# Attention chunks of 448 tokens, MLP blocks apart from them, and the last two MLP blocks beside each other

## The chip, the core and the metric

The kernel runs on one core of a Trainium2 chip. The metric is the device time of one execution in microseconds (us); before the change the median of three runs is 1187.18 us (1186.54 to 1188.1). TensorE (PE in the profile) multiplies, VectorE (DVE) and ScalarE (ACT) work on tiles element by element, GpSimd (POOL) helps a little, and SyncE (SP) issues the DMAs. Each engine works through its own instructions strictly in the order in which the program wrote them.

## The reference, cut to what matters

Batch 2, 3136 tokens each (6272 in all), 256 model columns. Three steps follow each other: an attention whose scores are squared and not normalised, an MLP with a convolution of three taps along the tokens, and a second MLP behind a LayerNorm.

```python
attn = np.maximum(z @ z.T / S, 0.0) ** 2          # z: 64 columns
x = u * (attn @ v)
h = np.maximum(x @ w_in, 0.0)                     # 1024 columns
c = conv_w[0]*h[t-1] + conv_w[1]*h[t] + conv_w[2]*h[t+1]
y = (h * sigmoid(c)) @ w_out
out = y + np.maximum(layernorm(y) * g_ln @ w_ch1, 0.0) @ w_ch2
```

## The kernel before, in words

Every float32 operand is split into a high and a low part that TensorE takes at full rate (`ah` and `al`, `vh` and `vl`, `gh` and `gl`), and a product is three matmuls: high by high, low by high, high by low.

The tokens are cut twice by `plan()` (L260). A *block* is what an MLP works on: 15 blocks of three tiles of 128 tokens and two of two tiles (`SIZES`). A *chunk* is what the attention works on; before the change there is one chunk per block, ending two tokens past it (the convolution needs one more token on either side), with exceptions at the border of the batches. The 17 chunks are 386, 384 six times, 446, 322, 384 six times, 256 and 256 wide.

Per chunk `c`, the attention goes through 25 tiles `j` of keys. `scores()` (L588) issues two matmuls into a PSUM bank of tag `w`; ACT takes the relu (L608) and the square (L617), or DVE squares (L613); ACT or DVE writes `ah` (L381, L385), DVE writes `al` (L626). `av()` (L648) then issues six matmuls (L658, L660, L661, for two halves of the columns) into the accumulator `av`. So a key tile costs eight matmuls of the chunk's width, and the last one six. `make_x()` (L669) multiplies by `u` and splits the result into `xh`, `xl`.

`mlps()` (L715) is one block: for each of eight slices `k` of the 1024 columns six matmuls into `hps` (L738 to L740), then relu, three taps, sigmoid and gate on ACT and DVE (L771 to L817), the split into `gh`, `gl`, and three matmuls of 256 columns per tile into the accumulator `y` (L754 to L756). After the eighth slice come the LayerNorm (ACT copy `ysb` L832, then DVE L837 to L872 with one power on POOL), the transposes `tps` (L884), and the second MLP with the same matmul counts (`h2ps`, `g2h`, `g2l`, `y`), a residual sum (L925) and the DMA out. The weights come in as 64-bit words and are decoded in 16 pieces of 512 columns (and a small one for the taps) by `decode()` (L477): about eight passes on DVE each, and three steps that ACT or POOL does between them.

What stands in which order is decided when the program is built. Every operation gets a due time; `Program.order()` (L144) plays the engines through with the prices of `PRICE` (L45), and each engine always takes the ready operation with the earliest due time whose buffers are free. `LAG0`, `LAG1` say how far an MLP's due times lie behind its chunk; `BESIDE` puts off the second MLP of the last block but one by 35 us.

Of the kernel before, what the change touches and what calls it, by code (L numbers as in the profile page):

```python
# [8 lines left out]
F32 = mybir.dt.float32  # L9
F32R = mybir.dt.float32r  # L10
U32 = mybir.dt.uint32
# [248 lines left out]
def plan():  # L260

    ends, t = [], 0
    for n in SIZES:
        t += n * P
        ends.append(t)
    assert t == NT
    chunks, blocks, q0, s = [], [], 0, 0  # L270
    for e in ends:
        q1 = NT if e == NT else e + 2
        if q0 < S < q1 or (q1 < S and S - q1 < 256):
            q1 = S
        if q1 == NT and q1 - q0 < 256:
            q0 = q1 - 256
            assert q0 >= s
        chunks.append((q0, q1))
        blocks.append((s, e))
        q0, s = q1, e  # L280
    return chunks, blocks
# [3 lines left out]
def attn_moe_kernel(ctx: ExitStack, tc: tile.TileContext, zt, ut, v, w_in, conv_w, w_out, g_ln, w1, w2, out):  # L285
    nc = tc.nc
    chunks, blocks = plan()
    NC = len(chunks)
# [3 lines left out]
    UW = max(q1 - s + 1 + (q1 == NT) for (_, q1), (s, _) in zip(chunks, blocks))  # L292
# [22 lines left out]
    def maker(tag, places, where, shape, dtype):  # L315
# [7 lines left out]
        for tag, places, where, shape, dtype in (  # L323
            ("zst", 2, pool, [P, 512], F32),
            ("st", 3, pool, [P, 1024], F32),
            ("wc", 2, pool, [P, 512], U32),
            ("wn", 2, pool, [P, 512], U32),
# [3 lines left out]
            ("a", 3, pool, [P, CW], F32),  # L331
# [13 lines left out]
            ("xtl", 1, pool, [P, 2 * BW], F32R),  # L345
            ("bst", 2, pool, [P, NTT, 6], F32),
# [222 lines left out]
    def head(c):  # L569

        return chunks[c][0] - blocks[c][0] + 1
# [97 lines left out]
    def make_x(c):  # L669
        q0, q1 = chunks[c]  # L670
        n, o = q1 - q0, head(c)
        w = blocks[c][1] - blocks[c][0] + 2
        u, b = u_b[c], av_b[c]
        xh, xl = x_b[c] = buf("xh", True), buf("xl", True)

        def half(t, d, a, e):
            return at(t).rearrange("p (k t) -> p k t", k=2)[:, d, a:e]
# [4 lines left out]
        if c == 0:  # L682
            op([("POOL", 0.15)], lambda e: nc.gpsimd.memset(edge(u, 0, 1), 0.0), writes=[(u, "head")], name="edge")
        else:
            k = head(c - 1) + chunks[c - 1][1] - chunks[c - 1][0]
            op(
                [("DVE", 0.09 + 0.0005 * 2 * o)],
                lambda e: nc.vector.tensor_copy(edge(u, 0, o), edge(u_b[c - 1], k - o, k)),
                reads=[(u_b[c - 1], 0), (u_b[c - 1], 1)], writes=[(u, "head")], name="edge", port=True,
            )  # L690
        keys = [(u, "head")]
        if q1 == NT:
            op([("POOL", 0.15)], lambda e: nc.gpsimd.memset(edge(u, o + n, o + n + 1), 0.0), writes=[(u, "tail")], name="edge")
            keys.append((u, "tail"))
        for d in range(2):
# [6 lines left out]
            )  # L702
        for d in range(2):
            op(
                ways_copy(w, "ACT"), lambda e, d=d: copy_r(e, half(xh, d, 0, w), half(u, d, 0, w)),
# [4 lines left out]
                lambda e, d=d: nc.vector.tensor_tensor(half(xl, d, 0, w), half(u, d, 0, w), f(half(xh, d, 0, w)), ALU.subtract),  # L710
                reads=[(u, d), (xh, d)] + keys, writes=[(xl, d)], name="xl", port=True,
            )


    def mlps(c, when):  # L715
        q0, q1 = chunks[c]
# [28 lines left out]
        def down(acc, nm, k, gh, gl, due):  # L745
            for i in range(ntt):

                def mm(e, i=i):
                    p = at(acc, "y").rearrange("p a b -> p (a b)")[:, i * D : (i + 1) * D]
# [4 lines left out]
                    nc.tensor.matmul(p, a, wh, start=first(acc, i // 2), stop=False, **kw)  # L754
# [5 lines left out]
                    adds=[(acc, i)], due=due + 0.3 * i, name=f"y{c}.{k}{nm}",  # L760
                )

        acc = buf("av", True) if last else buf("y", True)
# [60 lines left out]
        y = buf("u", True) if last else buf("ysb", True)  # L824
        bst, mv, ve, r, q = (buf(x) for x in ("bst", "mv", "ve", "rs", "rq"))

        def rows(i):
            return at(y)[:, i * D : (i + 1) * D]
# [39 lines left out]
        for i in range(ntt):  # L868
# [6 lines left out]
                reads=[(y, 0), (mv, i), (r, 1)], writes=[(xn, 0)], name="xn", port=True,  # L875
            )
            xns.append(xn)
        th, tl = (buf("xh", True), buf("xl", True)) if last else (buf("xth", True), buf("xtl", True))
        for d in range(2):
            ps = buf("w", kind="m")  # L880

            def turn(e, d=d, ps=ps):
# [10 lines left out]
                reads=[(ps, 0), ("gt",)], writes=[(th, d)], name="xth",  # L893
# [10 lines left out]
        acc2 = buf("y", True)  # L904
        for k in range(NF):
            ps = buf("w", kind="m")
            gh, gl = (buf("ah"), buf("al")) if beside else (buf("gh", True), buf("gl", True))
            for ways, fn, reads, due, d in up(ps, "w1", k, th, tl, n, when2(TURN + 0.02 + UP2 * k / NF)):
# [17 lines left out]
                at(y)[:, : ntt * D], at(acc2).rearrange("p a b -> p (a b)")[:, : ntt * D], at(y)[:, : ntt * D], ALU.add  # L926
            ),
            reads=[(acc2, i) for i in range(ntt)], writes=[(y, 0)], name="residual",
# [4 lines left out]
                in_=at(y)[:, : ntt * D].rearrange("p (i d) -> p i d", d=D),  # L933
            ),
            n, reads=[(y, 0)], due=when(1.1), name="out",
# [22 lines left out]
    last0 = max(c for c in range(NC) if chunks[c][1] <= S)  # L958
    for c in range(NC):
# [82 lines left out]
```

## Time and profile before

| what | value |
|---|---|
| median of three runs | 1187.18 us |
| the profiled execution, its own time | 1187.92 us |
| its span, first to last instruction | 1186.0 us |
| TensorE busy | 1157.5 us (98%), 7464 matmuls |
| VectorE, ScalarE busy | 847.4 us (71%), 856.4 us (72%) |
| mean granted TensorE clock | 0.996 of full speed |

The busy time of PE counts a matmul from its start to the end of its results, and consecutive matmuls overlap, so 98% busy is not 98% of what the engine could do: what a matmul costs in an unbroken run is the distance between two starts. A wait in brackets behind a row is idle time of that engine just before the instruction and what ended it.

### The profile page before, as it was taken

How to read it: one execution, taken by the hardware profiler on the slowest of the kernel's cores; microseconds unless marked ns; L12 is line 12 of the kernel's file. 1: busy time of each engine (PE TensorE's matmuls, PEld its weight loads, DVE VectorE, ACT ScalarE, POOL GpSimd, SP SyncE). 2: the span in 40 equal slices, each digit the busy share in tenths (PEclk: the TensorE clock that was granted, in tenths of full speed). 3: DMA queues.
4: the chain of work that ended last, by engine and by line, in shares of the span. 5: the costliest groups of instructions: out<-in, count | busy, mean ns of one | idle time of the engine just before them, and what ended most of it. 6: DMA issues, size and time to landing. Idle time of an engine off the chain costs nothing.

```text
span 1186.0 us, 19700 instructions
## 1 busy us (share of the span) xinstructions
PE 1157.5 (98%) x7464; PEld 1133.7 (96%) x7464; DVE 847.4 (71%) x1883; ACT 856.4 (72%) x1888; POOL 27.2 (2%) x39
## 2 busy tenths in 40 slices
PE   8899999999999999999999999999999999999996
PEld 7799899999999999999999999999999999999986
DVE  7999998758575777867585858675765748575764
ACT  7899886857676777868585857676767757686852
POOL 1000100000000000000000000000000000000000
PEclk9999999999999999999999999999999999999998
DMA  6421121001010012100000000000000000000000
GB/s 181 133 75 52 60 71 54 14 1 34 1 35 1 14 31 65 47 22 14 21 15 14 21 1 22 14 14 21 14 8 27 5 24 1 14 15 1 15 10 10
DMA packets 26127, 35.37 MB, mean 30 GB/s; under 512 B 2096, under 2 KB 21424, under 8 KB 26032
## 3 DMA queue, kind: packets, MB, share of 16 engines
q1 hardware_dynamic: 26032, 34.11, 9.6%
q8 instruction: 58, 0.95, 0.3%
q14 instruction: 37, 0.30, 0.1%
HBM read 24.67 MB, written 6.42 MB: 26 GB/s over the span
## 4 chain that ended last, share of the span: by engine, by line
PE 86%; DVE 6%; issue 4%; ACT 3%; DMA 0%; POOLq 0%; POOL 0%; DVEq 0%; ACTq 0%
PE av L660 10%; PE av L661 10%; PE av L658 10%; PE y L756 7%; PE y L754 7%; PE y L755 7%; PE s L599 5%; PE s L600 5%; PE h2ps L739 4%; PE h2ps L738 4%; PE h2ps L740 4%; PE hps L738 4%; PE hps L740 4%; PE hps L739 4%; DVE al L626 2%
## 5 line engine op out<-in xcount | busy, mean ns | idle before, releaser
L626 DVE TENSOR_TENSOR al<-a,ah 128x384 fp32r<-128x384 f32 (+4 forms) x408 | 218.3, 542 | 115.2 <-ACT ah L381 113.0
L658 PE MATMUL av<-ah,vh 128*128 128x384 f32 (+4 forms) x850 | 284.6, 335 | 8.4 <-ACT ah L381 6.5
L660 PE MATMUL av<-al,vh 128*128 128x384 f32 (+4 forms) x816 | 273.5, 335 | 7.3 <-DVE al L626 5.9
L661 PE MATMUL av<-ah,vl 128*128 128x384 f32 (+4 forms) x850 | 280.3, 330 | 0.0
L608 ACT ACTIVATE a<-s 128x384 f32<-128x384 f32 (+4 forms) x425 | 197.6, 477 | 107.6 <-PE s L600 104.8
L617 ACT ACTIVATE a<-a 128x384 f32<-128x384 f32 (+4 forms) x373 | 188.8, 512 | 5.3
L381 ACT CAST ah<-a 128x384 fp32r<-128x384 f32 (+4 forms) x345 | 171.1, 503 | 15.4 <-DVE a L613 9.0
L658 PEld LDWEIGHTS av<-ah,vh 128*128 128x128 f32 x850 | 160.5, 189 | 15.0 <-ACT ah L381 10.6
L660 PEld LDWEIGHTS av<-al,vh 128*128 128x128 f32 x816 | 154.2, 189 | 17.1 <-DVE al L626 16.3
L661 PEld LDWEIGHTS av<-ah,vl 128*128 128x128 f32 x850 | 160.4, 189 | 0.7
L599 PE MATMUL s<-hl 128*128 128x384 f32 (+4 forms) x425 | 141.0, 332 | 0.2 <-DVE hl L413 0.2
L600 PE MATMUL s<-lh,hl 128*128 128x384 f32 (+4 forms) x425 | 139.6, 329 | 0.0
L917 DVE SCALAR_TENSOR_TENSOR g2l<-h2ps,g2h 128x384 fp32r<-128x384 f32 (+1 forms) x136 | 73.2, 540 | 79.9 <-ACT g2h L912 78.9
L912 ACT ACTIVATE g2h<-h2ps 128x384 fp32r<-128x384 f32 (+1 forms) x136 | 64.9, 477 | 88.5 <-PE h2ps L740 86.9
L754 PE MATMUL y<-woh,gh 128*128 128x256 f32 x392 | 110.6, 282 | 0.9 <-DVE gh L385 0.8
L756 PE MATMUL y<-woh,gl 128*128 128x256 f32 x392 | 110.5, 282 | 0.6 <-DVE gl L816 0.6
L755 PE MATMUL y<-w2l,g2h 128*128 128x256 f32 x392 | 110.5, 282 | 0.0
L754 PE MATMUL y<-w2h,g2h 128*128 128x256 f32 x392 | 110.5, 282 | 0.0
L756 PE MATMUL y<-w2h,g2l 128*128 128x256 f32 x392 | 110.5, 282 | 0.0
L755 PE MATMUL y<-wol,gh 128*128 128x256 f32 x392 | 110.3, 281 | 0.0
L771 ACT ACTIVATE h<-hps 128x386 f32<-128x386 f32 (+1 forms) x136 | 65.2, 480 | 50.3 <-PE hps L740 49.2
L786 DVE SCALAR_TENSOR_TENSOR t<-h,cw,t 128x384 f32<-128x384 f32 (+1 forms) x136 | 81.8, 604 | 27.0 <-ACT t L777 25.7
(105 smaller groups left out, 2335.7 us busy)
## 6 DMA issues: line engine op xcount, KB each, us to landing
out_dram<-ysb SPq DMA_DIRECT2D x15, 384.0 KB, 2.5
vst<-in_v_dram SPq DMA_DIRECT2D x11, 512.0 KB, 3.9
u<-in_ut_dram SPq DMA_DIRECT2D x12, 384.0 KB, 3.2
wst<-in_w_dram SPq DMA_DIRECT2D x8, 512.0 KB, 3.8
zst<-in_zt_dram SPq DMA_DIRECT2D x12, 256.0 KB, 2.8
lh<-hl SPq DMA_DIRECT2D x24, 96.0 KB, 2.1
wst<-in_w_in_dram SPq DMA_DIRECT2D x4, 512.0 KB, 4.9
wst<-in_w_out_dram SPq DMA_DIRECT2D x4, 512.0 KB, 3.8
```

Of the source, the lines that this page charges most:

```text
L381: nc.scalar.copy(dst, src)
L599: nc.tensor.matmul(p, zj, hl[:, o : o + n], start=True, stop=False)
L600: nc.tensor.matmul(p, zj, at(lh)[:, :n], start=False, stop=True)
L608: [("ACT", price("act_ps", n))], lambda e: nc.scalar.activation(a(), at(ps)[:, :n], AF.Relu),
L617: op([("ACT", price("act", n))], lambda e: nc.scalar.activation(a(), a(), AF.Square), writes=[(ab, 0)], name="square")
L626: lambda e: nc.vector.tensor_tensor(at(al, "al")[:, :n], a(), f(at(ah)[:, :n]), ALU.subtract),
L658: nc.tensor.matmul(p, vhj, at(ah)[:, :n], start=first(b, d), stop=False, **kw)
L660: nc.tensor.matmul(p, vhj, at(al)[:, :n], start=False, stop=False, **kw)
L661: nc.tensor.matmul(p, vlj, at(ah)[:, :n], start=False, stop=False, **kw)
L754: nc.tensor.matmul(p, a, wh, start=first(acc, i // 2), stop=False, **kw)
L755: nc.tensor.matmul(p, a, wl, start=False, stop=False, **kw)
L756: nc.tensor.matmul(p, b, wh, start=False, stop=k == NF - 1, **kw)
```

## The change

The attention and the MLPs no longer share their cuts. Each batch gets seven chunks of 448 tokens (14 in all); the blocks stay as they were, and a block follows the first chunk that reaches past its end (`after`). The gate by `u` becomes a step of the chunk (`gate_u`), and `make_x` a step of the block that reads the gated `u` at an offset. The last two blocks (two tiles each) both follow the last chunk. They share the accumulator `av` for the first MLP, the accumulator `y` for the second and a buffer of tag `u` for the result, each in its own half (`i0`, `shared`); the second MLP of block 15 takes its input from the place of `hl`, which the scores no longer need. The due times of the second MLPs of blocks 14 and 15 are put off by 50 and 40 us (`DEFER`), and the lengths of the last blocks are set by hand. The lag falls to its floor by chunk 10 and not 12. To pay for the space, the decoding buffers `wc` and `wn` go from two places to one each; `a` goes from three to four.

```diff
+WIDTHS = [448] * 7
+LAG2 = 10
-BESIDE = 35.0
+LENGTH = 14.0, 14.0, 8.0, 8.0
+DEFER = 50.0, 40.0, 0.0
...
+    for n in WIDTHS * NB:
+        chunks.append((q0, q0 + n))
+        q0 += n
     for n in SIZES:
-        t += n * P
-        ends.append(t)
...
+        e = s + n * P
         blocks.append((s, e))
-        q0, s = q1, e
-    return chunks, blocks
+        after.append(next(c for c, (_, q1) in enumerate(chunks) if q1 > e or q1 == NT))
+        s = e
+    return chunks, blocks, after
...
-            ("wc", 2, pool, [P, 512], U32),
-            ("wn", 2, pool, [P, 512], U32),
+            ("wc", 1, pool, [P, 512], U32),
+            ("wn", 1, pool, [P, 512], U32),
-            ("a", 3, pool, [P, CW], F32),
+            ("a", 4, pool, [P, CW], F32),
...
+    def make_x(i):
+        s, e_ = blocks[i]
+        w, c = e_ - s + 2, after[i]
+        u, o = u_b[c], s - 1 - starts[c]
...
-        last, beside = c == NC - 1, c == NC - 2
+        tail, beside = c >= NK - 2, c >= NK - 3
         def when2(x):
-            return when(x) + (BESIDE if beside else 0.0)
+            return when(x) + DEFER[c - NK] if beside else when(x)
...
-        acc = buf("av", True) if last else buf("y", True)
+        i0 = 2 * (c - NK + 2) if tail else 0
+        acc = shared("av") if tail else buf("y", True)
-        y = buf("u", True) if last else buf("ysb", True)
+        y = shared("u") if tail else buf("ysb", True)
...
-        th, tl = (buf("xh", True), buf("xl", True)) if last else (buf("xth", True), buf("xtl", True))
+        if c == NK - 1:
+            th, tl = buf("xh", True), buf("xl", True)
+        elif tail:
+            th, tl = buf("zh"), buf("zl")
+            th.ap, tl.ap = hl[:, : 2 * n], hl[:, 512 : 512 + 2 * n]
+        else:
+            th, tl = buf("xth", True), buf("xtl", True)
-        acc2 = buf("y", True)
+        acc2 = shared("y") if tail else buf("y", True)
...
-        make_x(c)
-        lag = max(LAG1, LAG0 * (1 - c / 12))
-        length = NJ * step[min(c + 1, NC - 1)]
-        mlps(c, lambda x, c=c, lag=lag, length=length: 2 * (begin[c + 1] + lag + x * length))
+        gate_u(c)
+        for i in (i for i in range(NK) if after[i] == c):
+            make_x(i)
+            length = (blocks[i][1] - blocks[i][0]) / NT * begin[NC]
+            pace = max(pace, begin[c + 1])
+            if c >= NC - 2:
+                length = LENGTH[i - NK]
+            lag = max(LAG1, LAG0 * (1 - c / LAG2))
+            mlps(i, lambda x, pace=pace, lag=lag, length=length: 2 * (pace + lag + x * length))
+            pace += length
```

Most of what this does shows in the order alone. Three places follow (the number behind a name is the program's own count of its tiles, so it tells two tiles of one name apart).

**PE, end of chunk 11, before.** `s` are the scores, `ah`, `al` the parts made from them on ACT and DVE. The last row uses `ah_9925`, which is made from the score tile `s_9892`; the two matmuls of `s_9892` and the first one of `s_9897` stand right above the first row.

```order
L600 MATMUL s_9897<-lh_8133,hl_68 128x384
L658 MATMUL av_9134<-ah_9885,vh_69 128x384
L660 MATMUL av_9134<-al_9890,vh_69 128x384
L661 MATMUL av_9134<-ah_9885,vl_70 128x384
L658 MATMUL av_9134<-ah_9885,vh_69 128x384
L660 MATMUL av_9134<-al_9890,vh_69 128x384
L661 MATMUL av_9134<-ah_9885,vl_70 128x384
L599 MATMUL s_9915<-hl_68 128x384
L600 MATMUL s_9915<-lh_8133,hl_68 128x384
L658 MATMUL av_9134<-ah_9925,vh_69 128x384
```

**PE, end of chunk 11, in the change.** The last row uses `ah_10377`, made from `s_10340`; its two matmuls and the first one of `s_10345` stand right above.

```order
L601 MATMUL s_10345<-lh_8292,hl_68 128x448
L659 MATMUL av_9558<-ah_10330,vh_69 128x448
L661 MATMUL av_9558<-al_10338,vh_69 128x448
L662 MATMUL av_9558<-ah_10330,vl_70 128x448
L659 MATMUL av_9558<-ah_10330,vh_69 128x448
L661 MATMUL av_9558<-al_10338,vh_69 128x448
L662 MATMUL av_9558<-ah_10330,vl_70 128x448
L600 MATMUL s_10366<-hl_68 128x448
L601 MATMUL s_10366<-lh_9487,hl_68 128x448
L600 MATMUL s_10374<-hl_68 128x448
L601 MATMUL s_10374<-lh_9487,hl_68 128x448
L659 MATMUL av_9558<-ah_10377,vh_69 128x448
```

Before, ten matmuls of 384 columns lie between the score tile and its use; in the change twelve of 448, since two score tiles of the next chunk are issued here instead of one.

**PE, the last block between its two MLPs, before.** `y_14328` is the accumulator of its first MLP, `tps` are the transposes behind its LayerNorm, `h2ps` its second MLP.

```order
L754 MATMUL y_14328<-woh_73,gh_14475 128x256
L755 MATMUL y_14328<-wol_74,gh_14475 128x256
L756 MATMUL y_14328<-woh_73,gl_14477 128x256
L884 MATMUL tps_14505<-ident_64,xn_14501 128x128
L884 MATMUL tps_14505<-ident_64,xn_14503 128x128
L884 MATMUL tps_14508<-ident_64,xn_14501 128x128
L884 MATMUL tps_14508<-ident_64,xn_14503 128x128
L738 MATMUL h2ps_14517<-xh_14511,w1h_75 128x256
L739 MATMUL h2ps_14517<-xl_14514,w1h_75 128x256
L740 MATMUL h2ps_14517<-xh_14511,w1l_76 128x256
```

**PE, the same transposes of the last block in the change.** `y_13167` is the shared accumulator of the second MLPs; `h2ps<-hl` is the second MLP of block 15, whose input lies in `hl`.

```order
L766 MATMUL y_13167<-w2l_78,g2h_13157 128x256
L767 MATMUL y_13167<-w2h_77,g2l_13172 128x256
L765 MATMUL y_13167<-w2h_77,g2h_13157 128x256
L766 MATMUL y_13167<-w2l_78,g2h_13157 128x256
L767 MATMUL y_13167<-w2h_77,g2l_13172 128x256
L908 MATMUL tps_13218<-ident_64,xn_13201 128x128
L908 MATMUL tps_13218<-ident_64,xn_13206 128x128
L908 MATMUL tps_13221<-ident_64,xn_13201 128x128
L908 MATMUL tps_13221<-ident_64,xn_13206 128x128
L749 MATMUL h2ps_13226<-hl_68,w1h_75 128x256
L750 MATMUL h2ps_13226<-hl_68,w1h_75 128x256
L751 MATMUL h2ps_13226<-hl_68,w1l_76 128x256
```

Before, nothing stood between the last row of the first MLP and the transposes; now the second MLP of block 15 (45 matmuls of it since the last block's first MLP ended) stands there, and more of it behind the transposes.

**DVE, decoding of the weights (`wc`, `wn`), before.** The number behind `wc` tells the piece; `al` and `a` are the attention's.

```order
L493 TENSOR_SCALAR wc_722<-wc_722 128x512
L503 TENSOR_SCALAR wc_618<-wc_618 128x512
L494 TENSOR_SCALAR wc_722<-wc_722 128x512
L613 TENSOR_TENSOR a_739<-a_739,s_731 128x384
L516 TENSOR_TENSOR wol_74<-wn_614,wc_618 128x512
L495 TENSOR_SCALAR wc_722<-wc_722 128x512
L626 TENSOR_TENSOR al_765<-a_739,ah_755 128x384
L501 TENSOR_SCALAR wn_772<-wst_548 128x512
L613 TENSOR_TENSOR a_763<-a_763,s_752 128x384
L496 SCALAR_TENSOR_TENSOR wc_722<-wst_548,wc_722 128x512
L626 TENSOR_TENSOR al_793<-a_760,ah_783 128x384
L626 TENSOR_TENSOR al_800<-a_763,ah_786 128x384
```

**DVE, decoding in the change.**

```order
L495 TENSOR_SCALAR wc_849<-wc_849 128x512
L627 TENSOR_TENSOR al_911<-a_875,ah_903 128x448
L627 TENSOR_TENSOR al_918<-a_879,ah_906 128x448
L496 TENSOR_SCALAR wc_849<-wc_849 128x512
L502 TENSOR_SCALAR wn_928<-wst_521 128x512
L497 SCALAR_TENSOR_TENSOR wc_849<-wst_521,wc_849 128x512
L819 TENSOR_TENSOR t_828<-h_806,t_828 128x384
L503 SCALAR_TENSOR_TENSOR wn_928<-wst_521,wn_928 128x512
L504 TENSOR_SCALAR wc_849<-wc_849 128x512
L829 TENSOR_TENSOR gl_955<-t_828,gh_945 128x384
L799 SCALAR_TENSOR_TENSOR t_922<-h_913,cw_65,t_922 128x384
L517 TENSOR_TENSOR wil_72<-wn_928,wc_849 128x512
```

Before, pieces 618 and 722 run through each other; in the change a piece ends (`wil` is written) before the next one begins, and more of the attention and of the first MLP (`t`, `gl`) lies between.

## Rows read from the trace of the kernel before

**Rows 1.** The page: busy time, share of the span and instructions of each engine.

```profile
PE 1157.5 (98%) x7464; PEld 1133.7 (96%) x7464; DVE 847.4 (71%) x1883; ACT 856.4 (72%) x1888; POOL 27.2 (2%) x39
```

**Rows 2.** Busy time by stretch, first 200 us: length, busy time and count of each engine, TensorE clock.

```profile
20.00:60.00 40.00, 35.26 (x176) 30.17 (x176) 36.80 (x85) 33.27 (x75) 1.08 (x2) 1.00 0.47 142
60.00:100.00 40.00, 38.99 (x230) 37.52 (x229) 38.01 (x82) 35.30 (x79) 1.48 (x2) 1.00 0.21 64
100.00:160.00 60.00, 58.10 (x337) 55.22 (x336) 58.65 (x134) 51.22 (x114) 3.30 (x3) 1.00 0.20 58
160.00:200.00 40.00, 40.00 (x247) 40.00 (x246) 35.15 (x76) 29.93 (x66) 1.33 (x1) 1.00 0.24 68
```

**Rows 3.** Instructions in time on PE, three unbroken runs: start, duration, engine, line, tile, form.

```profile
562.53 0.28 PE L754 MATMUL y<-w2h,g2h 128*128 128x256 f32 x1
...
563.12 0.28 PE L756 MATMUL y<-w2h,g2l 128*128 128x256 f32 x1
...
300.13 0.34 PE L658 MATMUL av<-ah,vh 128*128 128x384 f32 x1
...
302.04 0.34 PE L661 MATMUL av<-ah,vl 128*128 128x384 f32 x1
...
484.21 0.37 PE L658 MATMUL av<-ah,vh 128*128 128x446 f32 x1
...
487.67 0.37 PE L600 MATMUL s<-lh,hl 128*128 128x446 f32 x1
```

**Rows 4.** Waits of PE between 200 and 1150 us: total us, times, longest.

```profile
PE av L658 <- ACT ah L381: 4.6, 6, 0.8
PE h2ps L739 <- DVE xtl L897: 1.1, 1, 1.1
```

**Rows 5.** Instructions in time, PE and ACT: the end of chunk 11, and of chunk 15.

```profile
800.71 0.80 ACT L832 COPY ysb<-y 128x768 f32<-128x768 f32 x1 [0.50 <-PE y L756]
...
802.42 0.33 PE L600 MATMUL s<-lh,hl 128*128 128x384 f32 x1
...
803.56 0.45 PE L658 MATMUL av<-ah,vh 128*128 128x384 f32 x1 [0.81 <-ACT ah L381]
...
804.43 0.34 PE L661 MATMUL av<-ah,vl 128*128 128x384 f32 x1
...
1129.45 0.28 PE L600 MATMUL s<-lh,hl 128*128 128x256 f32 x1
...
1130.97 0.28 PE L661 MATMUL av<-ah,vl 128*128 128x256 f32 x1
```

**Rows 6.** ACT by line and form: count, busy us, mean ns of one.

```profile
L608 ACT ACTIVATE a<-s 128x446 f32<-128x446 f32 x25 | 13.6, 542 | 13.6 <-PE s L600 13.6
L617 ACT ACTIVATE a<-a 128x446 f32<-128x446 f32 x25 | 14.5, 579 | 0.3
L381 ACT CAST ah<-a 128x446 fp32r<-128x446 f32 x22 | 12.5, 569 | 0.3
L491 ACT ACTIVATE wc<-wst 128x512 f32<-128x512 f32 x16 | 10.8, 679 | 0.6 <-DVE wil L516 0.4
```

**Rows 7.** Busy time by stretch at the end.

```profile
1152.57:1161.86 9.29, 7.82 (x50) 6.21 (x49) 8.40 (x23) 5.72 (x15) 0.00 (x0) 1.00 0.00 1
1161.86:1172.36 10.50, 6.67 (x30) 5.69 (x28) 4.31 (x15) 2.64 (x6) 0.69 (x1) 0.67 0.01 2
```

**Rows 8.** Waits of PE, whole span: the longest single one.

```profile
PE tps L884 <- DVE xn L872: 3.7, 1, 3.7
```

**Rows 9.** DVE by line and form: count, busy us, mean ns of one.

```profile
L626 DVE TENSOR_TENSOR al<-a,ah 128x384 fp32r<-128x384 f32 x288 | 157.8, 556 | 80.5 <-ACT ah L381 79.5
L786 DVE SCALAR_TENSOR_TENSOR t<-h,cw,t 128x256 f32<-128x256 f32 x16 | 7.7, 482 | 1.4 <-ACT t L777 1.4
L806 DVE TENSOR_TENSOR t<-h,t 128x256 f32<-128x256 f32 x16 | 6.8, 422 | 0.6 <-ACT t L801 0.2
L816 DVE TENSOR_TENSOR gl<-t,gh 128x256 fp32r<-128x256 f32 x16 | 6.8, 422 | 0.6
```

More of the change, by code (lines that the diff above doesn't have):

```diff
@@ L260, in plan @@
 def plan():
-    ends, t = [], 0
-    for n in SIZES:
-        t += n * P
-        ends.append(t)
[L269 to L278, printed above, removed]
+    chunks, blocks, after, q0, s = [], [], [], 0, 0
+    for n in WIDTHS * NB:
+        chunks.append((q0, q0 + n))
+        q0 += n
+    assert q0 == NT
+    for n in SIZES:
+        e = s + n * P
         blocks.append((s, e))
-        q0, s = q1, e
-    return chunks, blocks
+        after.append(next(c for c, (_, q1) in enumerate(chunks) if q1 > e or q1 == NT))
+        s = e
+    assert s == NT and set(after) == set(range(len(chunks)))
+    return chunks, blocks, after
 @with_exitstack
@@ L286, in attn_moe_kernel @@
     nc = tc.nc
-    chunks, blocks = plan()
-    NC = len(chunks)
+    chunks, blocks, after = plan()
+    NC, NK = len(chunks), len(blocks)
     CW = max(b - a for a, b in chunks)
     BW = max(b - a for a, b in blocks)
-    UW = max(q1 - s + 1 + (q1 == NT) for (_, q1), (s, _) in zip(chunks, blocks))
+    starts = [blocks[after.index(c)][0] - 1 for c in range(NC)]
+    UW = max(q1 - s + (q1 == NT) for (_, q1), s in zip(chunks, starts))
     XW = BW + 2
@@ L569, in head @@
     def head(c):
-        return chunks[c][0] - blocks[c][0] + 1
+        return chunks[c][0] - starts[c]
     def load_u(c):
@@ L709, in make_x, with shared @@
                 [("DVE", price("dve_2", w))],
-                lambda e, d=d: nc.vector.tensor_tensor(half(xl, d, 0, w), half(u, d, 0, w), f(half(xh, d, 0, w)), ALU.subtract),
+                lambda e, d=d: nc.vector.tensor_tensor(half(xl, d, 0, w), half(u, d, o, o + w), f(half(xh, d, 0, w)), ALU.subtract),
                 reads=[(u, d), (xh, d)] + keys, writes=[(xl, d)], name="xl", port=True,
             )
+    both = {}
+    def shared(tag):
+        if tag not in both:
+            both[tag] = buf(tag, True)
+        return both[tag]
     def mlps(c, when):
-        q0, q1 = chunks[c]
         s, e_ = blocks[c]
@@ L753, in mm @@
                     kw = {"skip_group_check": True}
-                    nc.tensor.matmul(p, a, wh, start=first(acc, i // 2), stop=False, **kw)
+                    nc.tensor.matmul(p, a, wh, start=first(acc, (i0 + i) // 2), stop=False, **kw)
                     nc.tensor.matmul(p, a, wl, start=False, stop=False, **kw)
@@ L925, in mlps @@
             lambda e: nc.vector.tensor_tensor(
-                at(y)[:, : ntt * D], at(acc2).rearrange("p a b -> p (a b)")[:, : ntt * D], at(y)[:, : ntt * D], ALU.add
+                flat(at(y)), flat(at(acc2).rearrange("p a b -> p (a b)")), flat(at(y)), ALU.add
             ),
-            reads=[(acc2, i) for i in range(ntt)], writes=[(y, 0)], name="residual",
+            reads=[(acc2, i0 + i) for i in range(ntt)], writes=[(y, i0)], name="residual",
         )
@@ L958, in attn_moe_kernel @@
     last0 = max(c for c in range(NC) if chunks[c][1] <= S)
+    pace = 0.0
     for c in range(NC):
```

41 lines of the change are left out of this document (22 added, 19 removed).

## The prediction

> **What bounds the kernel now.** I read the page first, then stretches, then single rows where a stretch is poor. The page has PE busy 98% of the span and DVE and ACT a little over 70% [rows 1], so PE is the bound on the whole; what the span holds beyond PE's own work must be found by stretch.
>
> The first 160 us are not PE's. From 20 to 160 us DVE is busy 36.8 + 38.0 + 58.65 = 133.5 of 140 us, and PE gets through 176 + 230 + 337 = 743 matmuls [rows 2]. What a matmul costs PE is the distance of starts in an unbroken run: 0.59 us over five steps of 256 columns (0.118), 1.91 over eleven of 384 (0.1736), 3.46 over seventeen of 446 (0.2035) [rows 3]. So 743 matmuls are at most 129 us even if all were 384 wide; some are narrower, and I put the loss at 13 us. In the next 40 us DVE is down to 35.15 and PE is unbroken.
>
> In the middle the trace names six waits of an `av` for an `ah` that ACT writes, 4.6 us together, and one of 1.1 for DVE [rows 4]. Idle time is not the whole price, since the first matmuls behind a wait come singly: from 802.42 to 804.43 three steps take 2.01 us and not 0.52, and at the last such place, 1129.45 to 1130.97, 1.52 and not 0.35 [rows 5]. That is 1.5 and 1.2 us lost, eight in all for six places at chunk ends; with the wait of 1.1 and a scatter of small ones I count 12. The reason stands in the same rows: ACT copies `ysb` (0.80 us) just where the next score tile waits for it.
>
> At the end, 50 matmuls (5.9 us) take 9.29 us while DVE is busy 8.40; then 30 (at most 3.5 us) take 10.50, at a mean granted clock of 0.67, that is partly at 1.2 and not 2.4 GHz [rows 7]. In the second stretch PE first stands idle 3.7 us, waiting for the LayerNorm of the last block [rows 8], and the low clock follows that. Lost: 3.4 + 7.0 = 10.4 us. The rest of the overhead (start, last residual and its DMA) is not touched.
>
> **A, wider chunks.** A chunk has 25 key tiles of eight matmuls less two, 198: 17 × 198 = 3366 become 14 × 198 = 2772, and the columns stay (6274 and 6272 per key tile). So only what a matmul costs apart from its columns goes. From 256 and 384 columns: 0.0556 us for 128 columns is 0.434 ns each, which leaves 6.8 ns per matmul; 594 × 6.8 ns = 4.0 us gained, 448 columns then costing 0.201 us. The run of 446 speaks against it: with two columns more it gives 0.2044, or 566.6 us for 2772 matmuls, against 563 for the old ones by the same rows: 3.5 us lost. Upwards I allow 8, since the intercept of two short runs is good to a factor of two. I take 4, from the rows of widths that are whole multiples of 64, as 448 is and 446 is not.
>
> The Trainium skill ("TensorE: Matmul & The Clock Gate", section "Back-to-back issue gap") gives an unthrottled matmul its columns at 2.4 GHz plus about 2.5 ns; by that the 594 matmuls would save only 1.5 us. No run of rows here is that short (0.1736 us against 0.1625 for 384), so the sum goes by the rows.
>
> **B, the head.** 75 fewer key tiles take three ACT steps and one on DVE each with them, but per column this relieves DVE little. What counts is the decoding. Counted over both orders, ahead of the place at which PE has some 122 us of matmuls behind it, DVE has eleven and a half pieces decoded before and nine and a half in the change; eight passes a piece at some 0.556 us (an `al` of 384, [rows 9]) make 9 us less DVE work there, 2 us of it given back by more of the MLP. The same work comes later, where DVE has room. I take 8 of the 13 us; what stays is the load of the first keys and values. Ends: 11, and 4 lost, for now one place each of `wc`, `wn` makes a piece wait for ACT's first step, 0.679 us [rows 6], behind the end of the last; a third of 16 such steps is 3.6 us. Queued behind such a wait on DVE are the `al` of the running chunk, so PE would wait for those.
>
> **C, chunk ends.** A score tile needs relu, square and split before its `av`: at 446 columns 0.542 + 0.579 + 0.569 = 1.69 us on ACT [rows 6], some 1.9 with the handovers between them (0.2, an estimate); at 384 the same chain is some 1.7. The order leaves 10 × 0.1736 = 1.74 us for it at the ends of chunks 11 to 14 now, and 12 × 0.201 = 2.4 us there in the change; I find only two places, both at the end of the last chunk, with less (1.8 and 2.0). Gained 10 of the 12, ends 5 and 11.
>
> **D, the end.** With both last blocks behind the last chunk, the LayerNorm of the last has 48 matmuls ahead of its transposes since its first MLP ended, 48 × 0.118 = 5.7 us against the 4.0 that the idle time and the last row took; PE does not fall idle, and so the clock should stay. Next in line is DVE: a slice of a first MLP costs it two taps and two products, 2 × 0.482 + 2 × 0.422 = 1.81 us [rows 9], against 12 × 0.118 = 1.42 on PE, which is why the first stretch of rows 7 is poor. In the change sixteen such slices (28.9 us) and eight `g2l` of block 14 (4.4) make 33.4 us on DVE, against 22.7 + 8 × 2.10 = 39.5 on PE. So PE leads, narrowly. I take 7 of the 10.4, ends 3 and 9.
>
> The other edits cost nothing: SP issues three `u` loads and three pairs of `lh` loads fewer, and none of the waits in rows 4 is for a DMA; gating per chunk does the same columns; a fourth place of `a` only widens the lead of the scores.
>
> Sum: 4 + 8 + 10 + 7 = 29. The profiled execution's span goes from 1186.0 to 1157, its own time from 1187.92 to 1159; the median lies 0.7 below that execution, so 1158 us.
>
> **Rivals.**
> *Columns alone.* PE's time is proportional to columns (A nothing, as the runs of 446 say), and DVE holds the head as before (B nothing): C and D leave 1187 − 17 = 1170. For it: DVE is over 95% busy in the head, and the same decoding has to be done. Against: the order moves it. The Trainium skill's section named under A, with its 1.5 us for A, lies close to this case.
> *The stalls move.* Where one wait is taken away in an order planned by fixed prices, the next operation is late: `al` on DVE at chunk ends, DVE at the end. Then C and D give only 3 and 2, and 1187 − 17 = 1170 as well; against it, the gaps in the order are wider nearly everywhere past 40 us, not at those places alone.
> *Decoding in single file* ends slower. If the three ACT steps of a piece are all exposed, 16 × 3 × 0.679 = 32.6 us of DVE idle time fall into the stretch where DVE is the bound [rows 6]. B is then a loss of 32.6; with A, C and D at 21 the time is 1187.2 + 32.6 − 21 = 1199. It decides from 21 / 16 = 1.3 us a piece on; below that the change still gains. For it: one place and an order that assumes each step on time. Against: between two pieces the order has other DVE work, an `al` or two at least.
> *The blocks do not overlap.* That the last two blocks run one behind the other is excluded by the order; the gain of D would be 0 and the time 1165.
>
> **How the numbers follow.** The forecast, 1149 to 1166, gets 0.70; the first two rivals (1166 to 1173) 0.20 together; single file 0.04; still faster than 1149 gets 0.06. All upper ends together (8 + 11 + 11 + 9 = 39) would be 1148, all lower ones (−3.5 − 4 + 5 + 3 = 0.5) the old time; neither is likely. The range 1149 to 1172 leaves out less than 2 in 10. A measurement of this kernel tells 0.2% (2.4 us) from no change; all cases but single file and the worst ends together are beyond it: faster 0.94, same 0.02, slower 0.04.
>
> **What would show it.** A: runs of 448 start 0.201 us apart (wrong at 0.204). B: from 20 to 160 us PE gets matmuls worth 132 us or more done, by the prices above, where it got 127. C: waits of `av` for `ah` between 200 and 1130 us under 1.5 us. D: no wait of `tps` above 0.5 us and a granted clock of 1.00 in the last 40 us but for the very end. The prediction is wrong if waits of `av` for `al` in the first 200 us grow past 15 us, or if DVE is busy throughout the last 100 us with PE waiting for `gh` and `gl`.

## The result, and the profile after

The change makes the kernel faster: 1152.6 us (median of four runs, 1152.26 to 1153.36) against 1186.86 beside it, a ratio of 0.971 with an interval of 0.9695 to 0.9729. The forecast was 1158 us, 1149 to 1172. The profiled execution's span goes from 1186.0 to 1150.3 us, 35.7 less. The page's line of busy times, to be held against [rows 1]:

```profile
PE 1136.2 (99%) x6870; PEld 1086.6 (94%) x6870; DVE 843.9 (73%) x1795; ACT 817.6 (71%) x1667; POOL 24.6 (2%) x39
```

There are 594 matmuls fewer, as counted. DVE's busy time is all but unchanged. To see where the 35.7 us come from, one needs what a matmul costs when nothing waits. The timeline of PE has a run of forty steps of 448 columns without other work between:

```profile
227.93 0.36 PE L661 MATMUL av<-al,vh 128*128 128x448 f32 x1
...
235.95 0.37 PE L601 MATMUL s<-lh,hl 128*128 128x448 f32 x1
```

8.02 us over 40 steps are 0.2005; over some thirty long runs it is 0.2013, from 0.200 to 0.202. With 0.2015 for 448, and 0.1742 and 0.1183 for the 384 and 256 of [rows 3], *lost time* below is the sum, over neighbouring matmuls, of what the distance of their starts exceeds the price of the first one's width, where it does so by more than 0.06 us (other widths by their own unbroken distances). So it counts idle time and slow restarts alike.

| kernel | lost, 0 to 160 us | of it 0 to 20 | lost, past 160 us | span |
|---|---|---|---|---|
| before | 23.4 | 7.9 | 26.2 | 1186.0 |
| after | 11.0 | 5.5 | 9.6 | 1150.3 |

The head gives 12.4 us, the rest 16.6; the 6.7 that are left of 35.7 are not lost time. Some 5 to 6 of them are the attention's matmuls (`s` and `av`): by the mean unbroken distance at each width they take 564.0 us before and 558 to 559 after. Half a microsecond is the shorter stretch behind the last matmul (4.4 us, then 3.9), and the rest scatter in the MLPs' matmuls. The 26.2 of before are 15.1 up to 1150 us (chunk ends) and 11.1 behind it (the end).

The windows of the head, beside [rows 2] (columns: stretch, its length, busy time of PE, PEld, DVE, ACT, POOL with instructions, granted clock, DMA share, GB/s):

```profile
20.00:60.00 40.00, 38.15 (x183) 33.65 (x183) 38.59 (x82) 31.87 (x66) 1.80 (x3) 1.00 0.45 135
60.00:100.00 40.00, 39.44 (x208) 36.81 (x207) 38.16 (x79) 37.33 (x79) 0.65 (x1) 1.00 0.19 55
100.00:160.00 60.00, 59.70 (x324) 55.83 (x323) 56.68 (x122) 49.64 (x103) 3.13 (x4) 1.00 0.19 57
```

DVE is busy 133.4 us in these 140, as before (133.5). Yet PE now gets 134.8 us worth of matmuls done (140 less the 5.5 lost, with a scatter of 0.3), where it got 125. That is 10.0 of the 12.4 us; the other 2.4 lie in the first 20 us, where the granted clock of the profiled execution was 0.91 before and is 1.00 after:

```profile
0.00:20.00 20.00, 16.07 (x71) 14.56 (x71) 13.02 (x24) 13.65 (x27) 2.79 (x10) 0.91 0.58 185
0.00:20.00 20.00, 16.20 (x72) 13.89 (x73) 15.83 (x29) 14.73 (x29) 1.58 (x9) 1.00 0.67 210
```

The windows of the end, which answer to [rows 7]:

```profile
1080.00:1100.00 20.00, 20.00 (x148) 19.70 (x147) 16.24 (x41) 14.76 (x38) 0.00 (x0) 1.00 0.00 1
1100.00:1120.00 20.00, 20.00 (x160) 20.00 (x160) 18.78 (x56) 14.56 (x39) 0.80 (x1) 1.00 0.01 2
1120.00:1140.00 20.00, 19.79 (x168) 19.59 (x167) 10.11 (x29) 7.08 (x19) 0.70 (x1) 1.00 0.06 20
```

PE waits 0.2 us once in these 60, and the clock stays at 1.00, its upper level of 2.4 GHz. The last matmul ends at 1146.4 us. The four longest waits of PE from 160 us to the end (engine, line, what it waited for; us in all, times, longest), beside [rows 4, 8]:

```profile
PE tps L908 <- ACT a L609: 1.3, 1, 1.3
PE av L661 <- DVE al L627: 1.2, 3, 0.5
PE av L659 <- DVE u L695: 0.5, 2, 0.3
PE av L659 <- ACT ah L382: 0.3, 1, 0.3
```

The waits for `ah` fell from 4.6 us to 0.3, and the 3.7 us for `xn` at the end are gone. But the first line is new. It is worth following, because the step named there, a relu on ACT, is not what PE waited for. The timeline around it, of PE and DVE:

```profile
894.86 0.36 PE L601 MATMUL s<-lh,hl 128*128 128x448 f32 x1
896.53 0.56 PE L908 MATMUL tps<-ident,xn 128*128 128x128 f32 x2 [1.31 <-ACT a L609]
...
894.44 0.63 DVE L695 SCALAR_TENSOR_TENSOR u<-av,u 128x448 f32<-128x448 f32 x1 [1.09 <-PE av L662]
894.98 0.15 DVE L876 TENSOR_TENSOR rq<-rs 128x3 f32<-128x3 f32 x1
895.17 0.16 DVE L877 SCALAR_TENSOR_TENSOR rq<-rq,ve 128x3 f32<-128x3 f32 x1
895.36 0.16 DVE L878 SCALAR_TENSOR_TENSOR rs<-rq,rs 128x3 f32<-128x3 f32 x1
895.44 0.62 DVE L695 SCALAR_TENSOR_TENSOR u<-av,u 128x448 f32<-128x448 f32 x1
895.98 1.05 DVE L888 TENSOR_SCALAR xn<-ysb,mv,rs 128x256 f32<-128x256 f32 x3
```

The transposes need `xn`, whose first row is done near 896.4. The relu ends at 896.49, just as the transposes begin (their first weight load at 896.50). Behind its other waits for ACT or DVE in this trace PE starts, in all cases but one, 0.04 us or more after the end of the step that is named. So a step that happens to end there has taken the name. The three small LayerNorm steps that `xn` needs stand on DVE behind the gate of the chunk, which itself waits 1.09 us for the chunk's last `av`, and between them and `xn` stands the gate's second half. So the stall of chunk 11's end was not removed: it became another one at the same place.

### The profile page after: what moved, and what is told of

Read it like the earlier page. It is cut to its first block, busy times and chain, and to the rows that moved or that the text cites. A ratio compares the mean times of both kernels' runs of the same rounds, so it can differ in the third digit from the quotient of the medians.

```text
span 1150.3 us, 18104 instructions
## 1 busy us (share of the span) xinstructions
PE 1136.2 (99%) x6870; PEld 1086.6 (94%) x6870; DVE 843.9 (73%) x1795; ACT 817.6 (71%) x1667; POOL 24.6 (2%) x39
## 4 chain that ended last, share of the span: by engine, by line
PE 94%; DVE 2%; ACT 2%; issue 1%; DMA 0%; POOL 0%; DVEq 0%; POOLq 0%
PE av L659 12%; PE av L662 12%; PE av L661 11%; PE y L767 8%; PE y L765 8%; PE y L766 8%; PE s L600 5%; PE s L601 5%; PE h2ps L749 4%; PE h2ps L750 4%; PE h2ps L751 4%; PE hps L749 4%; PE hps L750 4%; PE hps L751 4%; PE tps L908 1%
## 5 line engine op out<-in xcount | busy, mean ns | idle before, releaser
L627 DVE TENSOR_TENSOR al<-a,ah 128x448 fp32r<-128x448 f32 x336 | 206.4, 622 | 90.6 <-ACT ah L382 88.2
L609 ACT ACTIVATE a<-s 128x448 f32<-128x448 f32 x350 | 185.0, 542 | 111.7 <-PE s L601 111.3
L659 PE MATMUL av<-ah,vh 128*128 128x448 f32 x700 | 258.2, 369 | 3.6 <-ACT ah L382 1.6
L662 PE MATMUL av<-ah,vl 128*128 128x448 f32 x700 | 253.8, 363 | 0.0
L661 PE MATMUL av<-al,vh 128*128 128x448 f32 x672 | 245.4, 365 | 2.7 <-DVE al L627 2.7
L618 ACT ACTIVATE a<-a 128x448 f32<-128x448 f32 x298 | 170.5, 580 | 4.0
L382 ACT CAST ah<-a 128x448 fp32r<-128x448 f32 x273 | 152.6, 568 | 6.7 <-DVE a L614 2.5
L600 PE MATMUL s<-hl 128*128 128x448 f32 x350 | 128.3, 367 | 0.3 <-DVE hl L414 0.3
L601 PE MATMUL s<-lh,hl 128*128 128x448 f32 x350 | 128.0, 366 | 0.0
L799 DVE SCALAR_TENSOR_TENSOR t<-h,cw,t 128x384 f32<-128x384 f32 (+1 forms) x136 | 81.7, 603 | 17.1 <-ACT t L790 16.1
L749 PE MATMUL hps<-xh,wih 128*128 128x386 f32 (+1 forms) x272 | 90.7, 333 | 0.7 <-DVE a L614 0.6
```

The source lines that it names most:

```text
L600: nc.tensor.matmul(p, zj, hl[:, o : o + n], start=True, stop=False)
L601: nc.tensor.matmul(p, zj, at(lh)[:, :n], start=False, stop=True)
L609: [("ACT", price("act_ps", n))], lambda e: nc.scalar.activation(a(), at(ps)[:, :n], AF.Relu),
L618: op([("ACT", price("act", n))], lambda e: nc.scalar.activation(a(), a(), AF.Square), writes=[(ab, 0)], name="square")
L627: lambda e: nc.vector.tensor_tensor(at(al, "al")[:, :n], a(), f(at(ah)[:, :n]), ALU.subtract),
L659: nc.tensor.matmul(p, vhj, at(ah)[:, :n], start=first(b, d), stop=False, **kw)
```

## The experiments

Twelve kernels, each a small edit of the kernel before or of the change (but for the last version). All lost times are as defined above; "past 160" goes to the end. The twelfth, with chunks of mixed widths, stands in the text alone.

| kernel | median us | lost, 0 to 160 | lost, past 160 |
|---|---|---|---|
| change, three places of `a` | 1160.05 | 17.0 | 9.4 |
| change, three of `a`, two of `wc` | 1162.99 | 19.4 | 9.5 |
| before, one place of `wc`, `wn` | 1183.51 | 21.2 | 26.1 |
| before, four places of `a` | 1177.0 | 15.8 | 23.9 |
| before, both | 1176.25 | 12.2 | 27.1 |
| change, chunks of 392 | 1170.49 | 13.2 | 17.1 |
| change, nothing put off | 1169.49 | 11.5 | 25.9 |
| change, block 15 not put off | 1160.76 | 10.9 | 18.0 |
| change, lag to its floor by chunk 12 | 1151.72 | 10.9 | 8.8 |
| change, longer lag | 1146.42 | 9.8 | 6.2 |
| change, longer lag and other due times | 1144.9 | 9.5 | 4.0 |

### The head: places of `a`, places of `wc`

The change with three places of `a`:

```diff
-            ("a", 4, pool, [P, CW], F32),
+            ("a", 3, pool, [P, CW], F32),
```

> The changed kernel with three places of a instead of four, as before the change; all else stays. The prediction's theory: the gain of the head comes from decoding that stands later in the order, and the fourth place of a costs and gives nothing; then 1152.6 us, at most 2 us off. Rival: the fourth place is what gives the head its gain. In the order PE has, between 20 and 150 us of its own work, a mean of 4.6 us of matmuls between a key tile's scores and its av in the changed kernel and 4.0 here (3.4 before the change), so DVE's bursts of decoding make PE wait for al again, and of the 10 us that the stretch from 20 to 160 us gained more than half is lost: 1159 to 1162, with the matmuls between 20 and 160 us down and the rest of the span untouched.

1160.05 us, 7.4 above the change (ratio to before 0.977, 0.9753 to 0.979). The rival holds. Its windows from 20 to 60 us, and DVE's longest wait there:

```profile
20.00:60.00 40.00, 34.82 (x157) 28.23 (x155) 34.18 (x72) 30.80 (x64) 1.51 (x3) 1.00 0.43 133
DVE al L627 <- ACT ah L382: 3.1, 2, 2.5
```

PE is busy 34.8 us and not 38.15, and DVE 34.2 and not 38.6: *both* wait. DVE cannot be the bound of such a stretch. A place of `a` is held from the relu on ACT to the `al` on DVE, and a score tile needs one. So I read it as a round trip: with three places the scores lead by less, PE waits for `al`, and DVE for the next `ah`, which ACT makes from `a`. The busy share of the kernel before, over 95%, hid that. The runs show what the place is worth; the round trip itself is a reading of the waits.

The same place, given to the kernel before:

```diff
-            ("a", 3, pool, [P, CW], F32),
+            ("a", 4, pool, [P, CW], F32),
```

> The kernel before with four places of a, all else as before. The prediction's theory: no change, 1187 us within 1. Rival (the fourth place carries the gain of the head): the mean of PE work between scores and av in the head goes from 3.4 to 4.0 us, and 6 to 10 us of the 16 lost between 20 and 160 us go; besides, the order leaves 12 and not 10 matmuls of 384 columns ahead of the ah at the ends of chunks 11 to 14 (2.08 us against the chain's 1.9), so that part of the waits there goes too: 1175 to 1181. The end of the kernel keeps its 3.7 us wait for the LayerNorm.

1177.0 us, ratio 0.9917 (0.9902 to 0.9932): the rival again. 7.6 of the 9.8 us lie in the head, most of the rest at the ends of chunks 11 to 14, where a stall is 1.05 us and not 1.4.

One place each of the decoding buffers in the kernel before:

```diff
-            ("wc", 2, pool, [P, 512], U32),
-            ("wn", 2, pool, [P, 512], U32),
+            ("wc", 1, pool, [P, 512], U32),
+            ("wn", 1, pool, [P, 512], U32),
```

> The kernel before with one place each of the two decoding buffers, as in the change; all else as before. Rival 'decoding in single file' of the prediction: slower by up to 32.6 us, at 0.68 us per ACT step of a piece; the prediction's lower price for it was 3.6 us. The prediction's reading that the later decoding is what the head gains by: if one place alone makes the decoding later, 2 to 8 us faster. A third theory, that the places of the decoding do nothing because between two pieces DVE always has other work: within 2 us of 1187. I expect the third.

1183.51 us, ratio 0.9969 (0.9959 to 0.998). "Decoding in single file" has the wrong sign, and the third theory, which I expected, falls too: it is the second, 3.3 us faster. Two places of `wc` put back into the change, beside three of `a`:

```diff
-            ("wc", 1, pool, [P, 512], U32),
+            ("wc", 2, pool, [P, 512], U32),
...
-            ("a", 4, pool, [P, CW], F32),
+            ("a", 3, pool, [P, CW], F32),
```

> The changed kernel with two places of wc (the first decoding buffer) and three of a. Beside the run with three places of a alone (1160.05 us) it tells what the one place of wc does in the change. Theory after the run of the kernel before with one place each (3.3 us faster): one place holds the decoding back, so that it comes later and DVE has room for al in the head; two places bring 2 to 4 us back, all of it before 160 us: 1162 to 1164. Rival: with the wider chunks the order of the decoding no longer matters, 1160 within 1.

1162.99 us (1161.69 to 1164.04), 2.9 above the run with three of `a` alone (1158.31 to 1161.53); in the head 19.4 and 17.0 us are lost. What the place moves shows in how often ACT begins a piece (`abs`, L492) up to 160 us. With two places of `wc`:

```profile
L492 ACT ACTIVATE wc<-wst 128x512 f32<-128x512 f32 x14 | 9.4, 670 | 0.0
```

and with one, first with three places of `a`, then in the change:

```profile
L492 ACT ACTIVATE wc<-wst 128x512 f32<-128x512 f32 x11 | 7.5, 678 | 0.9 <-DMA lh<-hl 0.9
L492 ACT ACTIVATE wc<-wst 128x512 f32<-128x512 f32 x11 | 7.4, 677 | 1.2 <-DVE w1l L517 0.5 <-DVE clo L517 0.5 <-DVE wol L517 0.2
```

A piece now begins when the last step of the one before it (`w1l`, `wol`) frees the place, so eleven are begun and not fourteen. Which of the attention's steps DVE then does earlier is not shown: PE's waits for `al` up to 160 us are 4.3 us with two places and 4.2 with one. Last of this group, both edits of the places in the kernel before (the edits of the second and third diff together):

> The kernel before with one place each of the decoding buffers and four of a: all that the change does to places, without its chunks and blocks. If the two add up: 9.8 + 3.3 = 13.1 us from 1186.8, 1173.7. If both only give DVE's backlog of the head room, they share the gain and the second adds little: 1175.5 to 1177.5. Up to 160 us its lost time should then be that of the changed kernel, 10 to 13 us.

1176.25 us. In the head the two add up and a little more: 23.4 us lost become 12.2, as good as the change's 11.0, with the old chunks. But past 160 us it loses 27.1 and not 23.9, so the whole is only 0.75 us better than with `a` alone, little more than scatter. The stalls of chunks 11 to 14 stay as they are; 1.9 us of the 3.2 more lie between 160 and 220 us, most of it at 185 us, where the held-back decoding (`wc`, `w1h`) still stands on DVE and ACT beside the gate of a chunk. The rest is nearly all in the last blocks.

### The chunks: width and ends

```diff
-WIDTHS = [448] * 7
+WIDTHS = [392] * 8
```

> The changed kernel with eight chunks of 392 tokens per batch instead of seven of 448; blocks, places, the end and all else stay. 16 x 198 = 3168 av and score matmuls instead of 2772. By term A (6.8 ns per matmul apart from its columns) 396 x 6.8 ns = 2.7 us slower, 1155.3 with nothing else moving; if PE's time goes by columns alone, 1152.6. Rival: the width is also what keeps ACT and DVE ahead (a key tile of 448 gives PE 1.61 us against ACT's three steps of 1.69, one of 392 gives 1.41 us against some 1.5), so that waits of av between 160 and 1080 us come back: 5 to 8 us more, 1160 to 1164.

1170.49 us, ratio 0.9861 (0.9842 to 0.9879): slower than either theory. 18.2 us of span are 2.2 in the head, 7.5 past 160 us, and 8.4 in the matmuls themselves: 3168 × 0.1788 against 2772 × 0.2013 us, both from unbroken runs. Of the 7.5, four are the old stalls at their old places (802, 873, 944 and 1015 us, 1.0 each) and 2.1 are lost at 1127 us, behind the transposes of a late block. The timeline at the end of the first of these chunks:

```profile
802.19 0.33 PE L601 MATMUL s<-lh,hl 128*128 128x392 f32 x1
802.95 0.45 PE L659 MATMUL av<-ah,vh 128*128 128x392 f32 x1 [0.43 <-ACT ah L382]
803.55 0.44 PE L661 MATMUL av<-al,vh 128*128 128x392 f32 x1 [0.15 <-DVE al L627]
```

Two steps take 1.36 us and not 0.36, as in [rows 5]. So the fourth place of `a`, which is here, does not by itself take the `ah` waits away. Past 160 us PE's waits for `ah` on ACT are 4.6 us in the kernel before and 1.7 here; with four places in the kernel before, and with three places beside 448, they are

```profile
PE av L658 <- ACT ah L381: 2.3, 5, 0.5
PE av L659 <- ACT ah L382: 0.7, 1, 0.7
```

The last run has 0.5 more for `ah` made on DVE. So each helps, and the width helps more: place and width together leave 0.3. The matmul price stood off the line by which term A was worked out (0.1769 at 392), so one run reads it at several widths:

```diff
-WIDTHS = [448] * 7
+WIDTHS = [456, 440, 448, 464, 432, 450, 446]
```

> The changed kernel with chunks of 456, 440, 448, 464, 432, 450 and 446 tokens in each batch instead of seven of 448, to read the distance of starts by width in one trace. By the line through 256 and 384 columns (0.0556 us for 128) on which term A stands: 0.1943 at 432, 0.1978 at 440, 0.2004 at 446, 0.2012 at 448, 0.2021 at 450, 0.2047 at 456, 0.2082 at 464. If only whole multiples of 64 lie on that line, as the rows at 386, 392 and 446 suggest (0.177, 0.179, 0.2035), all but 448 are 0.002 to 0.003 higher; if multiples of 16 do, 432 and 464 lie on it and 440 and 456 above; if of 8, 392 should have been lower than it was. The kernel's own time is not the question; uneven chunks shift the order, 1150 to 1160.

One execution, 1160.06 us, at a granted clock of 1.00. Means of unbroken neighbours: 0.1963 at 432, 0.1999 at 440, 0.2031 at 446, 0.2032 at 448, 0.2053 at 450, 0.2073 at 456, 0.2101 at 464. No width lies on the line, and 448 no longer does either:

```profile
697.91 0.37 PE L659 MATMUL av<-ah,vh 128*128 128x448 f32 x1
...
703.62 0.36 PE L601 MATMUL s<-lh,hl 128*128 128x448 f32 x1
```

28 steps in 5.71 us, 0.2039, where the change has 0.2005 for the same instructions. That multiples of 64 are cheap is therefore not a property of the width alone. What else it hangs on (here the places of `ah`, `al` and the starts of the chunks lie elsewhere) was not tried. One more thing follows for term A. Width by width, the attention's matmuls take 564.0 us in the kernel before. With chunks of 392 there are 198 fewer of them, and they take 566.4 us; with the mixed widths there are 594 fewer, as in the change, and they take 564.4. So fewer matmuls alone did not make the attention cheaper in either run.

### The end: the put-off

```diff
-DEFER = 50.0, 40.0, 0.0
+DEFER = 50.0, 0.0, 0.0
```

> The changed kernel with block 14's second MLP put off by 50 us as in the change and block 15's not. By term D the 48 matmuls that cover the last LayerNorm are block 15's second MLP; without it the wait of tps (3.7 us or a little more) and the low clock of the end come back, but the first MLPs stay spread: 7 us, 1158 to 1162. Rival: block 14's second MLP covers it too, 1152.6 within 2.

1160.76 us, ratio 0.9781 (0.9766 to 0.9796), as term D has it. The timeline of PE at its end, and the window right behind:

```profile
1136.07 0.28 PE L767 MATMUL y<-woh,gl 128*128 128x256 f32 x1
1140.04 1.23 PE L908 MATMUL tps<-ident,xn 128*128 128x128 f32 x4 [3.69 <-DVE xn L888]
```

```profile
1140.00:1150.00 10.00, 9.82 (x60) 9.05 (x61) 3.35 (x8) 2.82 (x7) 0.00 (x0) 0.73 0.00 0
```

It is the wait of 3.7 us of [rows 8], and the clock behind it is low (0.73) as in [rows 7] (0.67). Nothing put off at all:

```diff
-DEFER = 50.0, 40.0, 0.0
+DEFER = 0.0, 0.0, 0.0
```

> The changed kernel with the second MLPs of blocks 14 and 15 put off by nothing (50 and 40 us in the change); the shared banks, the lengths and all else stay. By term D the put-off is what covers the LayerNorm of the last block: without it the transposes stand right behind the first MLP, PE waits 3.7 us or more for xn, the clock falls behind it, and the three first MLPs stand close together, so that DVE (1.81 us of taps and products per slice of two tiles against 1.42 us on PE) is the bound in them: all of the 10.4 us that D counted come back and up to 5 more, 1161 to 1168. Rival: the shared banks alone let the two blocks overlap, and the put-off is worth less than 4 us: 1153 to 1157.

1169.49 us, ratio 0.9849 (0.9835 to 0.9864), 1.5 above the expected range. Beside the wait for `xn` there are new ones (the five longest of PE past 160 us):

```profile
PE tps L908 <- DVE xn L888: 4.3, 2, 3.7
PE y L765 <- ACT gh L382: 2.8, 2, 1.6
PE av L661 <- DVE al L627: 1.8, 4, 0.6
PE tps L908 <- ACT a L609: 1.3, 1, 1.3
PE hps L749 <- ACT xh L382: 1.2, 1, 1.2
```

The first MLPs of the last blocks now follow each other, and in them DVE is the busiest engine; PE's 3.27 of 5 us here stand beside DVE's 4.97:

```profile
1105.00:1110.00 5.00, 3.27 (x26) 2.86 (x25) 4.97 (x15) 4.46 (x13) 0.00 (x0) 1.00 0.00 0
```

So the put-off of block 15 is worth 8.2 us, above all because it covers the last LayerNorm, and that of block 14 another 8.7, because it gives PE other work between the slices of the last first MLPs.

### The lag, and a version that beats both

```diff
-LAG2 = 10
+LAG2 = 12
```

> The changed kernel with the lag of the MLPs behind their chunks falling to its floor by chunk 12 and not 10, as before the change. The prediction gave this edit nothing. Theory: nothing in the first 160 us, where the lags of the first two chunks differ by at most 1 us; between 850 and 1000 us the LayerNorms fall elsewhere beside the chunk ends, which may move the waits of 1.5 and 0.8 us there either way: 1150 to 1154. Rival: the earlier MLPs are part of what the head gains, then 2 us slower or more.

1151.72 us (1151.37 to 1151.98), 0.9 below the change, less than the 0.2% that a measurement tells; the lost time goes the same way, from 9.6 to 8.8 past 160 us with nothing in the head. The prediction's nothing for this edit stands. A longer lag:

```diff
-LAG0 = 70.0
-LAG2 = 10
+LAG0 = 85.0
+LAG2 = 14
```

> A version to beat the change: the lag starts at 85 us and not 70, and falls to its floor by chunk 14 and not 10; all else as in the change. What the changed kernel still loses past 20 us are a few single places: waits at 23, 41, 53 and 71 us (3.5 us together), at 891 and 895 us (2.3), 962, 979 and 1071 (2.2). At 895 us PE waits for the transposes of a block whose three small LayerNorm steps stand on DVE behind the gate of the chunk (0.62 us), which itself waits for the chunk's last av. With MLPs that lag further, the order has no LayerNorm beside the gates of chunks 11 to 13. Expected 1145 to 1149. Rival: any other lag only shifts such places, 1152 to 1154; and the end may suffer, since more MLP work is left behind the last chunk.

1146.42 us, ratio 0.9658 (0.9644 to 0.9673). The waits of PE past 160 us are down to three lines, and that of the transposes at 895 us is not among them. Of the 4.6 us of lost time that go, 1.2 lie in the head, which the expectation did not name:

```profile
PE av L659 <- DVE u L695: 0.6, 2, 0.3
PE av L661 <- DVE al L627: 0.4, 2, 0.2
PE h2ps L750 <- DVE xtl L921: 0.3, 1, 0.3
```

The last version moves the due times further:

```diff
-LAG0 = 70.0
-LAG2 = 10
+LAG0 = 82.55
+LAG2 = 14
...
-UP1, DOWN1, TURN, UP2 = 0.4, 0.14, 0.6, 0.36
-LENGTH = 14.0, 14.0, 8.0, 8.0
-DEFER = 50.0, 40.0, 0.0
-HELP = 1.3
+UP1, DOWN1, TURN, UP2 = 0.4, 0.1455, 0.6563, 0.36
+LENGTH = 9.11, 6.7, 2.97, 3.45
+DEFER = 50.0, 58.88, 0.0
+HELP = 1.1103
...
-FUSED = 4, 2, 1
+FUSED = 2, 2, 1
...
-AFTER = {"PE": 0.2, "ACT": 0.165, "DVE": 0.15, "POOL": 0.13, "SP": 0.0}
+AFTER = {"PE": 0.2241, "ACT": 0.165, "DVE": 0.15, "POOL": 0.13, "SP": 0.0}
```

> A version to beat the change, further than the longer lag alone (1146.4 us): the lag starts at 82.55 us and reaches its floor by chunk 14; the transposes are due a little later (0.6563 of a block's length and not 0.6); the lengths of the last four blocks are 9.11, 6.7, 2.97 and 3.45 us, block 15's second MLP is put off by 58.9; VectorE squares every second score tile of the first two chunks and not of four; ScalarE and VectorE hand work to the other sooner. Same operations and widths, so PE's own work is that of the change. With the longer lag alone the trace still loses some 3 us past 160 us at chunk ends; this order leaves more matmuls there. Expected 1142 to 1145.5. Rival: the waits left by the longer lag are already the last that an order can take away: 1146.4 within 1.

1144.9 us (1144.84 to 1145.51), ratio 0.9649 (0.9636 to 0.9661), 7.7 below the change and 1.5 below the longer lag alone. One line of waits is left past 160 us:

```profile
PE av L659 <- DVE u L695: 0.7, 2, 0.4
```

Of 13.5 us still lost, 9.5 lie in the head, 5.5 of them in the first 20 us, while the first keys and values come in.

## Why the prediction was right, term by term

The sign and the order of size were right, and the median was missed by 5.4 us. That it came so near is in part luck: B came out larger than forecast and mostly by another cause than the one named, C came out at about half, and the errors offset each other.

- **A (4 forecast, 6.7 found, as what is left over; 5 to 6 of it in the attention's matmuls).** The count is right, 594 matmuls fewer, and so is the price of 448: a run at 0.2005 and a mean of 0.2013, where 0.201 was named. The size was off because the old side is dearer than the line through two short runs: 564.0 us for the attention's matmuls, where the line gives 561. That the fewer matmuls are the cause is not shown. The runs with 392 and with mixed widths have fewer matmuls than the kernel before too, and gain nothing (566.4 and 564.4 us). So the half of "Columns alone" that gives A nothing is not excluded; the half that gives B nothing falls, and with it the 1170. The rule of the Trainium skill that stood beside A, "TensorE: Matmul & The Clock Gate", section "Back-to-back issue gap", would give 448 columns 0.189 us, an estimate from it; the trace has 0.2005 and does not agree.
- **B (8 forecast, 12.4 found, 10.0 of it between 20 and 160 us).** The step that failed is its cause. "A fourth place of `a` only widens the lead of the scores" was costed at nothing, and it is the larger part: 6.0 us of the head in the change (17.0 to 11.0), 7.6 in the kernel before. The later decoding was read rightly, with 2.2 to 3.6 us lost less in the three pairs of runs, but its cause was not named: one place of `wc` does it, the very edit that the prediction feared. Width does next to nothing here: with the same places the old chunks lose 12.2 us and the new ones 11.0. And the reading under it, DVE as the bound of the head, was too simple: with three places of `a` DVE idles as well. The 13 us that B put there to be had were mis-sized too: by lost time they were 15.5, and the first 20 us, which were to stay, gave 2.4 more. The lower end of B, four lost to decoding in single file, was never near.
- **C (10 of 12 forecast, 5.5 found).** The waits of `av` for `ah` went from 4.6 to 0.3 us, as the order's wider gaps said; most of that is the width's, some the fourth place's. But the lost time up to 1150 us went only from 15.1 to 9.6, because "The stalls move", one of two rivals that had 0.20 together, came true by half: `tps` at 895 us, `al` at 891, 962 and 1071. The sign named for C, one kind of wait under 1.5 us, could not see this; the version with the longer lag, which has no wait of `tps` left and 0.4 us for `al`, shows that they were real.
- **D (7 of 10.4 forecast, 11.1 found, or 10.5 without the 0.6 that the change still loses in its last 36 us).** Mechanism right; both halves were seen in the runs without the put-off. The caution was not needed: DVE is busy 18.78 of 20 us at the worst and PE never waits long for it, for the deferred second MLPs lie between the slices. All of the 10.4 was to be had, and taking 7 of it was the mis-sized step.

6.7 + 12.4 + 5.5 + 11.1 = 35.7 of span, against 29 forecast: A, B and D were short by 11.2, C long by 4.5.

## What to carry to other kernels

A stretch in which one engine is 95% busy need not be bound by it: see whether a further buffer place, at the round trip that feeds it, lets both that engine and the one behind it do more. In an order planned beforehand, a stall that is removed can come back as another kind of wait at the same place, so measure lost time over the whole stretch and not the wait that you meant to remove. And when a last block's latency is covered by other work, take that work away in a run of its own, to see what it was worth.

## What was not expected of the hardware

The distance of starts at one and the same shape is not fixed: 448 columns cost 0.2005 us in the run shown of the change (0.2002 to 0.2023 over some thirty runs) and 0.2039 in the kernel with mixed widths, of which there is one execution, both at a granted clock of 1.00. By the means (0.2013 and 0.2032) that is 5 us over 2772 matmuls, nearly all of term A; its cause is open. And the list of waits names the event that came last before the start, whether or not PE needed it: at 895 us it names a relu on ACT, where the timeline has `xn` on DVE, held up by the gate.
